# Attention into softplus layer: another order of PSUM pools, two weight loads into the `part` buffer, and casts of the first weights in later units

## The chip, the cores and the metric

The kernel is one launch on one core of a Trainium2 chip. The metric is device time in microseconds; the kernel before was run three times. The engines are named as in the profile: PE (TensorE matmuls), PEld (its weight loads), DVE (VectorE), ACT (ScalarE), POOL (GpSimd) and SP (SyncE, which issues DMAs). Each engine runs its own list of instructions in order and waits on semaphores for the others.

## The reference

Three layers run one after the other, on 1152 tokens (2 batches of 576) with 512 features.

```
attention:  q,k rotated; scores = (q_rot @ k_rot^T)/sqrt(64); P = exp(scores - max);
            out = (P / (sum P + 1e-9)) @ v            # 2 batches, 8 heads, 576 rows, 64 features
x         = out transposed to (1152, 512)
layer 1:    h = x @ w_in (512x2048); g = max(h,0) + log1p(exp(-|h|)); x = g @ w_out (2048x512)
layer 2:    tokens with x @ w_skip > 0: expert e = argmax(x @ w_gate); x += gate * relu(x @ w1[e]) @ w2[e]
```

The weights arrive as 64-bit floats and are decoded on the chip; inputs to matmuls are kept as a high and a low part (`xh`, `xl`; the two halves of a `w` tile), and a product is three matmuls.

## The kernel before

**Attention** (`Attention.run`) goes over units `(b, hp, u)`: batch, pair of heads, a chunk of 128 rows. In each unit PE makes scores `s`, DVE takes their maximum `m`, ACT makes `P` by exp, PE transposes `P` into PSUM tiles `t`, ACT and DVE copy these to `pt`, and PE multiplies `pt` with the values (`pv`, from `vd` and `vr`). When a chunk is done, PE transposes the normalisation (`t..n`), ACT copies it to `rb`, DVE multiplies `x = pv * rb`, and POOL splits `x` into `xh` and `xl`. There is one PSUM buffer for `pv`, so the next chunk's first `pv` matmul waits until DVE has read the last one. The order is written out by hand within a unit.

Beside the units run **jobs on the first weights** of layer 1. `W_AT` gives, for weight `(f, x)` (f a slice of 128 hidden columns; x is 0 for `w_in`, 1 for `w_out`), the numbers of the units at whose end each job is issued: load, first decode, second decode, `high`, `low`. `decode` is three DVE instructions on 128x512 (raw to `wt`; lines 557, 558, 560), `high` is an ACT cast of `wt` into `w` (line 565), `low` a DVE subtraction (line 569). The jobs of later weights are placed by `Moe1.weights`, in program order with a scheduler.

**Layer 1** walks over steps (chunk of tokens, f). `hidden` issues 12 matmuls of 512 columns per PSUM tile of 512 tokens (`h000` is chunk 0, f=0; `h010` f=1; line 591), then on ACT `y`=abs, `r`=relu, exp, `d`, `u`=ln (lines 604 to 614), on DVE three additions into `d` and `r` (615 to 617), on ACT the cast `gh` and on DVE `gl`. `out_mm` adds three matmuls for each of four token tiles into `acc` (line 629), and runs two steps behind `hidden`: the PE order is h000, h010, h020, h030, acc for f=0, h040, acc for f=1, h050, and so on. `hidden` has two PSUM buffers (pool `hp`), so h020 waits until ACT has read h000 twice (`y`, `r`).

Pools take memory in the order in which they are opened, and layer 1's lie where attention's were: the first writer of a new tile waits for the last reader or writer of the old one. Before, the PSUM pools of attention are opened `ps_s`, `ps_t`, `ps_pv`, and h000 lies in a slot of `ps_t` whose last tile is `t13n1`, the normalisation of the last chunk. In both kernels the tile `w2` lies where the values `vd` were, so that the cast `w2<-wt20` on ACT waits for the first `pv131<-pt131,vd1` matmul. The raw weights of 512 KB go through a ring `st` of two buffers. Layer 2 (`Moe2`) follows on the same engines.

Of the kernel before, what the change touches and what calls it, by code (L numbers as in the profile page):

```python
# [11 lines left out]
F32 = mybir.dt.float32  # L12
# [8 lines left out]
PSUM = bass.MemoryType.PSUM  # L21
# [17 lines left out]
SMALL = {1: ("l0",), 2: ("x0", "h0"), 3: ("t0", "r0"), 4: ("l1",), 5: ("x1", "h1"), 6: ("t1", "r1")}  # L39

W_AT = (
    ((0, 0), (18, 24, 25, 25, 26)), ((0, 1), (20, 26, 27, 27, 28)), ((1, 0), (25, 28, 29, 29, 30)),
    ((1, 1), (27, 30, 31, 31, 32)), ((2, 0), (29, 32, 33)), ((3, 0), (31, 34, 35)), ((2, 1), (33, 36, 37)),
)

WARM = (15, 4, 4, 3, 6, 3)

# [481 lines left out]
class Moe1:  # L529
# [6 lines left out]
        self.w, self.raw, self.t = {}, {}, {}  # L536


    def load(self, f, x):
        raw = self.raw[f, x] = self.st.tile([128, 512], mybir.dt.int64, name=f"raw{f}{x}", tag="st", bufs=2)  # L540
        fs = slice(128 * f, 128 * f + 128)
        if x == 0:
            src = self.w_in[:, fs].rearrange("(k p) n -> p k n", p=128)
            self.nc.sync.dma_start(raw.rearrange("p (k n) -> p k n", k=4), src)
        else:
            self.nc.sync.dma_start(raw, self.w_out[fs, :])
# [23 lines left out]

    def weights(self, f, x, wp, bufs, after):
        if (f, x) not in self.t:
            self.load(f, x)
            with after():
                self.decode(f, x, 0)
                self.decode(f, x, 1)
        with after():
            self.high(f, x, wp, bufs)
            self.low(f, x)
# [814 lines left out]
def const_views(ct):  # L1394
    return dict(
        ident=ct[:, 0:128], iota=ct[:, 128:256], wts=ct[:, 272:280], row1=ct[:, 280:289],
        far=ct[:, 289:290],
    )


def rope_views(cr):
    return dict(
        cos=cr[:, 0:256], sin=cr[:, 256:512], cosr=cr[:, 512:576], sinr=cr[:, 576:640],
    )
# [11 lines left out]
def attention_moe_moe_kernel(ctx: ExitStack, tc, q, k, v, w_in, w_out, w_skip, w_gate, w1, w2, tab, out):  # L1416
    nc = tc.nc

    def pool(stack, name, bufs=1, space=None, **kw):
        if space is not None:  # L1420
            kw["space"] = space
        return stack.enter_context(tc.tile_pool(name=name, bufs=bufs, **kw))
# [10 lines left out]
    with ExitStack() as s1:  # L1433
        xp = pool(s1, "xp")
        xh = xp.tile([128, 4, NTOK], F32R, name="xh")
        xl = xp.tile([128, 4, NTOK], F32R, name="xl")
        st = pool(s1, "st")
        moe1 = Moe1(nc, w_in, w_out, xh, xl, st)
        with ExitStack() as s2:
            nat, wq, wp, wk = pool(s2, "nat"), pool(s2, "wq"), pool(s2, "wp"), pool(s2, "wk")  # L1440
            ps = [pool(s2, "ps_s", 2, PSUM), pool(s2, "ps_t", 3, PSUM), pool(s2, "ps_pv", 1, PSUM)]
            cr = nat.tile([128, 640], F32, name="cr")
            nc.scalar.dma_start(cr, tab[:, 0:640])
            nc.scalar.dma_start(ct, tab[:, 640:930])
            cst = const_views(ct)
            cst.update(rope_views(cr))
            att = Attention(tc, q, k, v, cst, xh, xl, (nat, wq, wp, wk, *ps))

            def side(i):
                for (f, x), at in W_AT:  # L1450
                    for k, job in enumerate((moe1.load, moe1.decode, moe1.decode, moe1.high, moe1.low)[: len(at)]):
                        if at[k] == i:
                            job(f, x, **({"z": k - 1} if 0 < k < 3 else {"wp": wa, "bufs": 2} if k == 3 else {}))

            att.run(side)
# [8 lines left out]
        moe2.ring = [(wa, 2), (wc, 4)]  # L1464
        psa, accb = pool(ctx, "psa", 1, PSUM), pool(ctx, "accb", 2, PSUM)
        with ExitStack() as s2:
            gq, gp = pool(s2, "gq"), pool(s2, "gp")
            ring = [(wa, 2), (pool(s2, "wb0"), 3), (pool(s2, "wb1"), 2), (wc, 4)]
            tp = pool(s2, "tp")
            hp, accp = pool(s2, "hp", 2, PSUM), pool(s2, "accp", 3, PSUM)  # L1470
            cf = tp.tile([128, 512], F32, name="cf", tag="x2", bufs=5)[:, 0:256]
            nc.scalar.dma_start(cf, tab[:, 930:1186])
            nc.vector.tensor_copy(cb, cf)

            part = tp.tile([128, 4, 512], F32, name="part")
            ranges = ((0, 0, 6), (1, 0, 16), (2, 6, 16), (3, 6, 16))
            steps = [(ph, ci, f) for ph, (ci, f0, f1) in enumerate(ranges) for f in range(f0, f1)]
            due, pend, accs = [], [], {}
# [39 lines left out]
            for ph, ci, f in steps:  # L1518
# [20 lines left out]
                if (ph, f) in EARLY:  # L1539
                    c = EARLY.index((ph, f))  # L1540
                    raw = st.tile([128, 1024], F32, name=f"wr{c}", tag="st", bufs=2)
# [26 lines left out]
    with ExitStack() as s1:  # L1568
        wp, xp, ws = pool(s1, "wr"), pool(s1, "xp2"), pool(s1, "ws")
# [4 lines left out]
        ps = pool(s1, "ps_x", 2, PSUM), pool(s1, "ps_y", 1, PSUM), ((accb, "acc"), (pool(s1, "ps_h", 2, PSUM), "mh"))  # L1574
# [48 lines left out]
```

## Time and profile before

| what | value |
|---|---|
| median of 3 runs | 492.97 us (492.56 to 493.24) |
| the profiled execution | 493.06 us |
| its span | 491.2 us |
| mean granted PE clock | 0.998 |
| PE, DVE, ACT, POOL busy | 96%, 76%, 68%, 27% of the span |

The span is what the trace covers; about 1.9 us of the execution's own time lie around it. PE is busy nearly always, so that what counts is where PE has gaps, and which engine ends them.

### The profile page before, as it was taken

How to read it: one execution, taken by the hardware profiler on the slowest of the kernel's cores; microseconds unless marked ns; L12 is line 12 of the kernel's file. 1: busy time of each engine (PE TensorE's matmuls, PEld its weight loads, DVE VectorE, ACT ScalarE, POOL GpSimd, SP SyncE). 2: the span in 40 equal slices, each digit the busy share in tenths (PEclk: the TensorE clock that was granted, in tenths of full speed). 3: DMA queues.
4: the chain of work that ended last, by engine and by line, in shares of the span. 5: the costliest groups of instructions: out<-in, count | busy, mean ns of one | idle time of the engine just before them, and what ended most of it. 6: DMA issues, size and time to landing. Idle time of an engine off the chain costs nothing. (4 is left out here: it accounts for less than half of the span.)

```text
span 491.2 us, 8838 instructions
## 1 busy us (share of the span) xinstructions
PE 471.3 (96%) x3054; PEld 382.1 (78%) x3055; DVE 371.8 (76%) x699; ACT 332.3 (68%) x782; POOL 130.6 (27%) x166
## 2 busy tenths in 40 slices
PE   7999999999999999999999999999999999999994
PEld 3777777766777678999998898899897768677683
DVE  7666776688996796799988995454886688979563
ACT  2667776676877677876678677765685458957550
POOL 0966785766131400000000000000110152551002
PEclk9999999999999999999999999999999999999999
DMA  7477547458462240223344241420335545895231
GB/s 186 152 194 195 121 123 200 95 161 208 101 177 77 97 129 1 87 63 113 125 129 125 91 129 44 140 75 2 99 100 203 228 111 194 285 311 224 78 120 39
DMA packets 41509, 65.49 MB, mean 133 GB/s; under 512 B 9087, under 2 KB 23679, under 8 KB 41456
## 3 DMA queue, kind: packets, MB, share of 16 engines
q1 hardware_dynamic: 38480, 59.99, 40.0%
q0 software_dynamic: 1344, 4.20, 2.7%
q10 hardware_dynamic: 1632, 0.66, 0.6%
q8 instruction: 26, 0.43, 0.4%
q14 instruction: 27, 0.22, 0.1%
HBM read 67.32 MB, written 6.76 MB: 151 GB/s over the span
## 5 line engine op out<-in xcount | busy, mean ns | idle before, releaser
L591 PE MATMUL h<-xh,w 128*128 128x320 f32 (+2 forms) x464 | 104.2, 309 | 0.8 <-ACT rb L96 0.8
L629 PE MATMUL acc<-w,gh 128*128 128x512 f32 x288 | 80.8, 397 | 1.3 <-ACT gh L619 1.3
L591 PEld LDWEIGHTS h<-xh,w 128*128 128x128 f32 x464 | 78.1, 188 | 4.7 <-ACT rb L96 1.1
L591 PE MATMUL h<-xl,w 128*128 128x320 f32 (+2 forms) x232 | 69.2, 308 | 0.0
L270 DVE TENSOR_REDUCE m<-s 128x1 f32<-128x576 f32 x64 | 48.0, 754 | 19.5 <-PE s L261 16.1
L629 PEld LDWEIGHTS acc<-w,gh 128*128 128x128 f32 x288 | 51.8, 188 | 12.0 <-ACT gh L619 3.2
L283 ACT ACTIVATE P<-s,m 128x576 f32<-128x576 f32 x64 | 47.6, 749 | 12.3 <-DVE m L270 10.7
L705 POOL TENSOR_SCALAR sc<-lg 128x2 f32<-128x2 f32 (+1 forms) x3 | 0.9, 293 | 201.8 <-DVE lg L688 201.8
L973 DVE TENSOR_TENSOR ws<-raw,ws 128x1024 fp32r<-128x1024 f32 x42 | 49.4, 1219 | 6.6 <-ACT ws L966 6.1
L604 ACT ACTIVATE y<-h 128x320 f32<-128x320 f32 (+2 forms) x58 | 25.4, 438 | 41.1 <-PE h L591 39.9
L352 PE MATMUL t<-ct,P 128*128 128x128 f32 x288 | 45.5, 277 | 2.5 <-ACT pt L96 2.5
L629 PE MATMUL acc<-w,gl 128*128 128x512 f32 x144 | 45.9, 392 | 0.0
L966 ACT CAST ws<-raw 128x1024 fp32r<-128x1024 f32 x42 | 42.0, 1051 | 5.2 <-DMA raw<-in_moe_w_dram 5.0
L620 DVE TENSOR_TENSOR gl<-r,gh 128x256 fp32r<-128x256 f32 (+2 forms) x42 | 25.8, 614 | 26.0 <-ACT gh L619 25.8
L261 PE MATMUL s<-ks,qs 128*128 128x288 f32 x224 | 43.7, 317 | 1.8 <-ACT P L283 1.7
L591 PEld LDWEIGHTS h<-xl,w 128*128 128x128 f32 x232 | 43.2, 188 | 2.0
L352 PEld LDWEIGHTS t<-ct,P 128*128 128x128 f32 x288 | 33.6, 140 | 9.6 <-issue 3.5
L96 ACT COPY pt<-t 128x384 f32<-128x384 f32 x60 | 28.1, 480 | 18.0 <-PE t L352 17.9
L396 PE MATMUL pv<-pt,vr 128*64 128x256 f32 (+1 forms) x256 | 37.1, 412 | 0.0
L638 PE MATMUL y<-ws,hT 128*128 128x512 f32 (+1 forms) x150 | 37.0, 392 | 0.0
L261 PEld LDWEIGHTS s<-ks,qs 128*128 128x128 f32 x224 | 31.6, 189 | 6.6 <-ACT P L283 3.6
L638 PE MATMUL mh<-ws,xgT 128*128 128x512 f32 x132 | 36.6, 418 | 0.0
(305 smaller groups left out, 946.1 us busy)
## 6 DMA issues: line engine op xcount, KB each, us to landing
raw<-in_moe_w_dram SPq DMA_DIRECT2D x56, 512.0 KB
raw<-in_moe_w_in_dram SPq DMA_DIRECT2D x16, 512.0 KB
raw<-in_moe_w_out_dram SPq DMA_DIRECT2D x16, 512.0 KB
sraw<-in_moe_w_dram SPq DMA_DIRECT2D x16, 512.0 KB
ks<-kT SPq DMA_DIRECT2D x28, 288.0 KB
qs<-qT SPq DMA_DIRECT2D x28, 128.0 KB
wr<-in_moe_w_dram SPq DMA_DIRECT2D x5, 512.0 KB
x2d<-x SPq DMA_DIRECT2D x9, 256.0 KB
```

The costliest lines, as they stand in the source:

```text
L96: self.nc.scalar.copy(out, in_)
L261: nc.tensor.matmul(ps[:, c, 0:288], lhsT=qs[:, a, uc], rhs=ks[:, a, x, 288 * c : 288 * c + 288], start=x == 0, stop=x == 1,)
L270: self.last = nc.vector.tensor_reduce(st["m"][:, a : a + 1], st["ps"][a][:, :, 0:288], axis=AX.XY, op=ALU.max, negate=True)
L283: nc.scalar.activation(P[:, 576 * a : 576 * a + 576].rearrange("p (c n) -> p c n", c=2), ps[:, :, 0:288], AF.Exp, bias=m[:, a : a + 1], ac ...
L352: self.tail = nc.tensor.transpose(ps[:, 128 * i : 128 * i + 128], src, ident)
L396: nc.tensor.matmul(ps[r, 0:n], lhsT=v, rhs=pt[:, k, 0:n], start=i < 0, stop=i == 3, skip_group_check=True,)
L591: nc.tensor.matmul(ps[c][:, 0:m], lhsT=w[:, 0, x, 128 * k : 128 * k + 128], rhs=src[:, k, c0 + m * c : c0 + m * c + m], start=z == 0, stop ...
L620: self.last = nc.vector.tensor_sub(gl, r, gh.bitcast(F32))
L629: nc.tensor.matmul(acc[t], lhsT=g[x][:, 128 * j : 128 * j + 128], rhs=w[:, 1, y, :], start=f == f0 and z == 0, stop=f == f1 and z == 2,)
L638: mm()
L966: self.nc.scalar.copy(self.w[T, c][:, 0], self.raw[c] if raw is None else raw)
L973: self.nc.vector.tensor_sub(w[:, 1], self.raw[c] if raw is None else raw, w[:, 0].bitcast(F32))
```

## The change

It has three parts. (1) The PSUM pool `ps_t` is opened ahead of `ps_s`, so that the first `h` tiles lie where scores were. (2) Pool `tp` is opened ahead of `gq` and `gp`; a tile `px` of two raw buffers takes the memory that `part` uses later, and the raw loads of weights (5,0) and (4,1) are issued into it at the start of layer 1 and not through the ring `st`. (3) In `W_AT` two casts `high` and four subtractions `low` move to later units.

```
 W_AT = (
-    ((0, 0), (18, 24, 25, 25, 26)), ((0, 1), (20, 26, 27, 27, 28)), ((1, 0), (25, 28, 29, 29, 30)),
-    ((1, 1), (27, 30, 31, 31, 32)), ((2, 0), (29, 32, 33)), ((3, 0), (31, 34, 35)), ((2, 1), (33, 36, 37)),
+    ((0, 0), (18, 24, 25, 25, 27)), ((0, 1), (20, 26, 27, 28, 29)), ((1, 0), (25, 28, 29, 30, 31)),
+    ((1, 1), (27, 30, 31, 31, 33)), ((2, 0), (29, 32, 33)), ((3, 0), (31, 34, 35)), ((2, 1), (33, 36, 37)),
 )
+PX = ((5, 0), (4, 1))
...
-    def load(self, f, x):
-        raw = self.raw[f, x] = self.st.tile([128, 512], mybir.dt.int64, name=f"raw{f}{x}", tag="st", bufs=2)
+    def load(self, f, x, raw=None):
+        if raw is None:
+            raw = self.st.tile([128, 512], mybir.dt.int64, name=f"raw{f}{x}", tag="st", bufs=2)
+        self.raw[f, x] = raw
...
         if (f, x) not in self.t:
-            self.load(f, x)
+            if (f, x) not in self.raw:
+                self.load(f, x)
...
-            ps = [pool(s2, "ps_s", 2, PSUM), pool(s2, "ps_t", 3, PSUM), pool(s2, "ps_pv", 1, PSUM)]
+            ps_t, ps_s, ps_pv = pool(s2, "ps_t", 3, PSUM), pool(s2, "ps_s", 2, PSUM), pool(s2, "ps_pv", 1, PSUM)
...
+            tp = pool(s2, "tp")
             gq, gp = pool(s2, "gq"), pool(s2, "gp")
             ring = [(wa, 2), (pool(s2, "wb0"), 3), (pool(s2, "wb1"), 2), (wc, 4)]
-            tp = pool(s2, "tp")
             hp, accp = pool(s2, "hp", 2, PSUM), pool(s2, "accp", 3, PSUM)
+            px = tp.tile([128, 2, 512], mybir.dt.int64, name="px", tag="part")
+            for z, at in enumerate(PX):
+                moe1.load(*at, raw=px[:, z])
...
-            part = tp.tile([128, 4, 512], F32, name="part")
+            part = tp.tile([128, 4, 512], F32, name="part", tag="part")
```

The number behind a name in the rows of order below is only a count of tiles.

First place: ACT in attention, where chunk `t10n1` is normalised, before:

```order
L283 ACTIVATE P11m_1697,sm111_1698<-s11m0_1683,m11m_1694 128x576
L288 COPY P11m_1697<-P11m_1697 128x64
L565 CAST w0_1587<-wt01_1646 128x512
L96 COPY rb101_1727<-t10n1_1719 128x256
L96 COPY rb101_1727<-t10n1_1719 64x64 x2
```

and in the changed kernel (lines are some lower there by the added code):

```order
L285 ACTIVATE P11m_1696,sm111_1697<-s11m0_1682,m11m_1693 128x576
L290 COPY P11m_1696<-P11m_1696 128x64
L98 COPY rb101_1726<-t10n1_1718 128x256
L98 COPY rb101_1726<-t10n1_1718 64x64 x2
L98 COPY pt110_1613<-t1132_1722 128x3x128
L98 COPY pt111_1743<-t11m0_1748 128x4x64 x2
L285 ACTIVATE P110_1757,sm111_1697<-s1100_1738,m110_1753 128x576
L285 ACTIVATE P110_1757,sm111_1697<-s1101_1759,m110_1753 128x576
L569 CAST w0_1587<-wt01_1645 128x512
```

The cast of weight (0,1) stood ahead of the two copies of `rb101`; now it stands behind two exps. On DVE the subtraction `w0<-wt00` now stands just ahead of the second decode of `wt01` and of `x101`, and the subtraction `w0<-wt01`, which stood ahead of the next decodes, now stands behind two maxima.

Second place: PE at the end of attention (`t1312` is the last transposed `P`, `pv131` the last chunk's output). Before:

```order
L352 MATMUL t1311_2333<-ct_65,P131_2293 128x128 x3
L352 MATMUL t1312_2338<-ct_65,P131_2293 128x128 x3
L396 MATMUL pv131_2351<-pt131_2244,vd1_105 64x320 x2
L396 MATMUL pv131_2351<-pt131_2244,vr13_1782 64x320 x8
L316 MATMUL t13n1_2365<-ct_65,R131_2348 128x128 x3
L591 MATMUL h000_2441<-xh_74,w0_1587 128x512
L591 MATMUL h000_2441<-xl_75,w0_1587 128x512
```

In the changed kernel (the 12 matmuls of h000 begin right behind `t1312`, and these rows begin at the last of them):

```order
L596 MATMUL h000_2444<-xh_74,w0_1587 128x512
L596 MATMUL h010_2475<-xh_74,w1_1867 128x512
L596 MATMUL h010_2475<-xl_75,w1_1867 128x512
L596 MATMUL h010_2475<-xh_74,w1_1867 128x512 x2
L596 MATMUL h010_2475<-xl_75,w1_1867 128x512
L596 MATMUL h010_2475<-xh_74,w1_1867 128x512 x2
L596 MATMUL h010_2475<-xl_75,w1_1867 128x512
L398 MATMUL pv131_2351<-pt131_2244,vd1_105 64x320 x2
L398 MATMUL pv131_2351<-pt131_2244,vr13_1781 64x320 x8
L318 MATMUL t13n1_2365<-ct_65,R131_2348 128x128 x3
L596 MATMUL h010_2475<-xh_74,w1_1867 128x512 x2
```

All 12 matmuls of h000 and 8 of the 12 of h010 now stand ahead of `pv131`; before, all of them stood behind `t13n1`.

Third place: ACT at the same point of the program, before:

```order
L96 COPY pt131_2244<-t1312_2338 128x3x128
L565 CAST w2_2435<-wt20_1983 128x512
L565 CAST w3_2438<-wt30_2081 128x512
L565 CAST w2_2435<-wt21_2173 128x512
L96 COPY rb131_2369<-t13n1_2365 128x256
L96 COPY rb131_2369<-t13n1_2365 64x64 x2
L1472 DMA cf_2431<-in_constants_dram 128x256
L565 CAST w4_2507<-wt40_2503 128x512
L565 CAST w3_2438<-wt31_2512 128x512
L604 ACTIVATE y00_2454<-h000_2441 128x512
L606 ACTIVATE r00_2455<-h000_2441 128x512
L608 ACTIVATE y00_2454<-y00_2454 128x512
```

and in the changed kernel:

```order
L98 COPY pt131_2244<-t1312_2338 128x3x128
L569 CAST w2_2438<-wt20_1982 128x512
L569 CAST w3_2441<-wt30_2081 128x512
L609 ACTIVATE y00_2457<-h000_2444 128x512
L611 ACTIVATE r00_2458<-h000_2444 128x512
L569 CAST w2_2438<-wt21_2173 128x512
L613 ACTIVATE y00_2457<-y00_2457 128x512
L1482 DMA cf_2434<-in_constants_dram 128x256
L98 COPY rb131_2369<-t13n1_2365 128x256
L98 COPY rb131_2369<-t13n1_2365 64x64 x2
L617 ACTIVATE d00_2465<-y00_2457 128x512
L619 ACTIVATE u00_2459<-y00_2457 128x512
```

The casts `w2` and `w3` still come right behind the last `pt131` copy; `y00` and `r00` now stand right behind them, ahead of `rb131`, and the second cast of `w2`, and those of `w4` and `w3`, later. On DVE the subtraction `w2<-wt20` still is the first instruction behind the last `pt131` copy. From it up to and with the third addition `r01` (which the `gh` cast for f=1 waits for) there are 31 instructions before and 30 in the changed kernel; the set is the same but for one subtraction `w4<-wt41`, which now comes behind `r01`. From h100 on, layer 1 has the same order in both kernels, and so has what is executed of layer 2.

## Rows read from the trace of the kernel before

**Rows 1.** Busy time by stretch: PE, PEld, DVE, ACT, POOL, clock, DMA share, GB/s.

```profile
200.00:300.00 100.00, 100.00 (x566) 91.29 (x565) 88.79 (x139) 73.67 (x194) 0.00 (x0) 1.00 0.36 111
400.00:491.00 91.00, 84.01 (x549) 63.90 (x547) 66.20 (x83) 55.62 (x79) 24.51 (x14) 0.99 0.51 176
```

**Rows 2.** Timeline of chunk `t10n1` in attention: start, us, engine, line, operation, [idle before, releaser].

```profile
115.41 0.55 PE L316 MATMUL t10n<-ct,R 128*128 128x128 f32 x3
115.46 0.75 DVE L560 SCALAR_TENSOR_TENSOR wt<-raw,wt 128x512 uint32<-128x512 uint32 x1
...
116.24 0.62 ACT L565 CAST w<-wt 128x512 fp32r<-128x512 f32 x1 [1.17 <-DVE wt L560]
...
116.77 0.69 ACT L96 COPY rb<-t10n 128x256 f32<-128x256 f32 x3
117.28 0.76 DVE L270 TENSOR_REDUCE m<-s 128x1 f32<-128x576 f32 x1 [1.08 <-PE s L261]
...
117.96 0.48 DVE L405 TENSOR_TENSOR x<-pv,rb 128x320 f32<-128x320 f32 x1
...
118.50 0.65 PE L396 MATMUL pv<-pt,vd 128*64 128x256 f32 x4 [0.66 <-DVE x L405]
```

**Rows 3.** Busy time by stretch around it.

```profile
116.00:120.00 4.00, 3.08 (x25) 1.99 (x23) 2.88 (x7) 3.68 (x11) 3.92 (x5) 1.00 1.00 225
...
124.00:128.00 4.00, 3.11 (x26) 2.68 (x25) 3.97 (x9) 3.52 (x10) 2.34 (x4) 1.00 0.46 135
```

**Rows 4.** Timeline from the end of attention into layer 1.

```profile
160.87 0.76 PE L396 MATMUL pv<-pt,vd 128*64 128x320 f32 x4
...
161.67 1.66 ACT L565 CAST w<-wt 128x512 fp32r<-128x512 f32 x3 [0.42 <-PE pv L396]
162.32 1.29 DVE L569 TENSOR_TENSOR w<-wt,w 128x512 fp32r<-128x512 f32 x2 [1.64 <-ACT w L565]
...
163.71 0.55 PE L316 MATMUL t13n<-ct,R 128*128 128x128 f32 x3
...
165.09 0.50 PE L591 MATMUL h<-xh,w 128*128 128x512 f32 x1 [0.84 <-ACT rb L96]
...
175.88 0.39 PE L591 MATMUL h<-xh,w 128*128 128x512 f32 x1
```

**Rows 5.** Timeline: POOL's split of `x`, alone and beside DVE.

```profile
154.49 0.46 POOL L100 TENSOR_SCALAR xh<-x 128x320 fp32r<-128x320 f32 x1 [0.91 <-DVE x L405]
...
155.03 0.87 POOL L407 TENSOR_TENSOR xl<-x,xh 128x320 fp32r<-128x320 f32 x1
...
166.58 1.63 POOL L100 TENSOR_SCALAR xh<-x 128x320 fp32r<-128x320 f32 x1 [4.90 <-DVE x L405]
...
167.81 2.23 DVE L569 TENSOR_TENSOR w<-wt,w 128x512 fp32r<-128x512 f32 x2
...
168.30 1.20 POOL L407 TENSOR_TENSOR xl<-x,xh 128x320 fp32r<-128x320 f32 x1
...
169.59 0.88 POOL L776 TENSOR_SCALAR gt<-least 128x40 f32<-128x40 f32 x3
```

**Rows 6.** Timeline: DVE's two waits for raw loads, and its `r01`.

```profile
171.09 0.43 DVE L557 TENSOR_SCALAR wt<-raw 128x512 uint32<-128x512 uint32 x1 [1.04 <-DMA raw<-in_moe_w_in_dram]
...
177.18 0.43 DVE L557 TENSOR_SCALAR wt<-raw 128x512 uint32<-128x512 uint32 x1 [0.38 <-DMA raw<-in_moe_w_out_dram]
...
181.25 0.69 DVE L617 TENSOR_TENSOR r<-r,d 128x512 f32<-128x512 f32 x1
```

**Rows 7.** Timeline of PE: first `acc` matmuls for f=0 and for f=1.

```profile
176.90 2.14 PE L629 MATMUL acc<-w,gh 128*128 128x512 f32 x8 [0.64 <-ACT gh L619]
...
182.65 2.14 PE L629 MATMUL acc<-w,gh 128*128 128x512 f32 x8
```

**Rows 8.** Busy time from DVE's `w2<-wt20` to its `r01`.

```profile
162.32:181.83 19.51, 18.04 (x84) 13.81 (x81) 18.01 (x31) 13.88 (x27) 3.83 (x7) 1.00 0.37 117
```

**Rows 9.** Timeline of SP: the raw load of weight (5,0).

```profile
167.12 0.37 SPq L544 DMA_DIRECT2D raw<-in_moe_w_in_dram  x1
```

More of the change, by code (lines that the diff above doesn't have):

```diff
@@ L1446, in attention_moe_moe_kernel @@
             cst.update(rope_views(cr))
-            att = Attention(tc, q, k, v, cst, xh, xl, (nat, wq, wp, wk, *ps))
+            att = Attention(tc, q, k, v, cst, xh, xl, (nat, wq, wp, wk, ps_s, ps_t, ps_pv))
             def side(i):
```

## The prediction, made before the changed kernel was run

> **What bounds the kernel now.** First the busy time by stretch: PE is busy without a gap over the 100 us of layer 1 after its start, and loses 7 us in the last 91 us [rows 1]. A delay or a gain ahead of 200 us is therefore carried to the end, if layer 2 absorbs nothing of it (I take that it doesn't; nothing in layer 2 is moved). So only PE's gaps ahead of 200 us can be won or made, and I read the timeline at the two places that the change moves: one chunk of attention at 115 to 119 us, and the passage into layer 1 from 160 to 185 us. Every time below that is not "before" is an estimate made from these rows.
>
> **Attention: the casts in other units.** The subject is `x`, since PE's next `pv` waits for it: `pv` starts at 118.50, released by DVE's `x` of 117.96, which ran 0.48 [rows 2]. `x` needs `rb`, three copies of together 0.69 from 116.77, and these stood behind a cast of 0.62 at 116.24, which waited 1.17 for DVE's decode. `t10n` itself was there at 115.41 + 0.55 = 115.96 [rows 2]. In the changed order the cast stands behind, so `rb` can run from about 116.0 to 116.7. On DVE one subtraction now goes ahead of the decode: 0.60, which is what a second instruction of such a pair adds (1.29 for two [rows 4], 0.69 for one [rows 6]). Decode at 116.06, `x` from about 116.7 to 117.2, `pv` from 117.3 where PE is free. That is up to 1.2 earlier, but PE has only 4.00 - 3.08 = 0.92 idle in this stretch to give back [rows 3]. **Term 1: -0.9.** DVE fills with this subtraction what was idle (1.08 before `m` at 117.28 [rows 2]), so that its total does not grow. Bounds: PE's other gap nearby, 4.00 - 3.11 = 0.89 [rows 3], lies where DVE is busy 3.97 of 4 us; if the freed DVE time closes that too, -1.8. If the subtraction ahead of `x` is held up by POOL as one of the pair below is (0.94/2 = 0.47), -0.45.
>
> **PSUM order: what it removes.** Before, h000 waits for `rb` and starts at 165.09, with 0.84 of PE idle ahead of it [rows 4]. Where scores lay, the last reader is long done, and h000 starts right behind the last transposes, at about 160.8. That much is a pure gain: h000 is 4.3 earlier.
>
> **What it moves.** The same 20 hidden matmuls now stand ahead of `pv131`. One costs (175.88 - 165.09)/47 = 0.230, from the first and the last of 48 [rows 4]; 20 of them 4.6. So `pv131` starts at about 165.4 where it was 160.87: 4.5 later. Behind `pv131` hangs the cast `w2` on ACT, at 161.67 before, released by `pv` [rows 4]; and on it DVE's `w2` subtraction, at 162.32, released by the cast [rows 4]. Both are 4.5 later: 166.2 and 166.8. Queued behind them on ACT are `y00` and `r00`, and on DVE all of the decoding of w4, w3 and w5 and the additions for f=0 and f=1. PE earns 4.3 us of early matmuls and DVE stands still for as long.
>
> **Whether DVE then sets the end.** The last instruction that matters on DVE is `r01`: ended at 181.25 + 0.69 = 181.94 [rows 6], and the `acc` matmuls for f=1 came 0.71 later, at 182.65, with no gap on PE [rows 7]. So before, DVE was just in time there, with nothing in hand. From `w2` to `r01` it took 181.94 - 162.32 = 19.62, of which 19.51 - 18.01 = 1.50 was idle [rows 8], chiefly the two waits for raw loads, 1.04 and 0.38 [rows 6]. Those two go (next part), and one subtraction (0.60) moves behind `r01`: 17.5 are left. From 166.8 this ends at 184.3, and `acc` for f=1 starts at 185.0 and not at 182.65: +2.4. DVE may start a little earlier than by this sum, since h000 meets a running PE; I take **term 2: +2.2**.
>
> **The bounds of term 2.** In the 17.5 there is a collision. DVE's pair at 167.81 took 2.23 and not 1.29, while POOL split `x` in 1.63 and 1.20, which took 0.46 and 0.87 at 154.49 and 155.03 [rows 5]. DVE lost 0.94. In the changed kernel POOL's split again falls into DVE's dense run (behind `x131`, at about 172), so I keep it; without it +1.3. Upward: POOL's three `gt` instructions (0.88 [rows 5]) may lie beside DVE as well; by half their time, 0.44, and with the split costing DVE POOL's whole 0.46 + 0.87 = 1.33, it is +3.0.
> The Trainium skill ("SBUF — State Buffer", section "Who interferes with whom") says that a DVE instruction with two SBUF inputs and a GpSimd instruction that reads SBUF exclude each other through a shared port, the later one blocked for all of the other. By that rule the loss would be 1.33 and the sum below 0.4 higher; the trace agrees that both sides suffer, and shows 0.94.
>
> **The loads into `part`.** They wait for the last matmul that reads `vr13`, at about 165.4 + 2.8 = 168.2 (`pv131` takes up to `t13n1`, 163.71 - 160.87 [rows 4]). A load took 171.09 - 167.12 = 3.97 from issue to DVE's use [rows 6, 9], so the first lands at about 172.2. DVE wants it as its 12th instruction, at about 173.9, and the second two microseconds and more after that. They cost nothing: 1.7 of DVE work cover them, and if that cover is gone each 0.1 of lateness is 0.1 at `r01`. Through the ring the load would wait for `wt40` to be decoded, about 171.2, and land at 175.2, 1.3 too late; so this part earns what the sum leaves out. On SP the load of (5,1) stands behind both; it needs a ring buffer that DVE frees at about 171, and is wanted at 178. The moved pool and the extra tile add no instruction.
>
> **The rest of the passage.** h020 waits for `r00`: casts of 1.66/3 = 0.55 each [rows 4] from 166.2, then `y00` and `r00`, to about 168.5; PE gets there at 165.4 + 3.4 + 0.9 = 169.7 (`pv131` and `t13n1` took 163.71 + 0.55 - 160.87 [rows 4], then 4 matmuls of h010). No wait. h030 waits for `r01` of ACT, at about 172.8 against 172.4. The `acc` matmuls for f=0 come at about 177.4, against 176.90 with 0.64 idle [rows 7]; all of that lies inside the wait at f=1 and isn't added.
>
> **Sum.** -0.9 + 2.2 = +1.3 on the profiled execution's 493.06 us, which is 0.09 above the median of the three runs. On the median that is 494.3 us. About 0.2% (1 us) is what a measurement of this kernel can tell from no change.
>
> **The rivals.**
> - *No change to be seen.* The mechanism is as above, but POOL's split does not cost DVE its 0.94 (+1.3), or attention gives both gaps back (-1.8): with one of the two +0.4, with both -0.5, so 492.5 to 493.4. For it: POOL was the one that lost more in rows 5. Against: DVE is denser there than before. With half of either it is +0.8, still unseen. Chance 0.40.
> - *Faster.* The cast `w2` does not hang on `pv131` any more, because the pools that were reordered put `w2` elsewhere. Then ACT and DVE start as before, `r01` is not late, and PE keeps what it loses now, 0.84 ahead of h000 and 0.64 ahead of `acc` [rows 4, 7]: -1.5 - 0.9 = -2.4, 490.6 us. It decides from the point where DVE's `w2` starts before about 164.6 (the 2.2 given back). Against: the cast follows the same copies in both orders, and its old memory is still that of the values. Chance 0.09.
> - *Much slower.* The split and `gt` block DVE wholly (+3.0) and attention returns 0.45: +2.5, 495.5 us. Against: the measured pair lost less. Chance 0.13, within the slower side.
> - *Weights late.* The loads into `part` are behind on SP, and DVE waits at `wt50` again, 1.04 as before [rows 6]: +2.3, 495.3 us. Chance 0.05.
>
> **Numbers.** The forecast, +1.3 with its own spread of +1.0 to +1.9, has 0.33; with the two slower rivals slower has 0.51, no visible change 0.40, faster 0.09. The range leaves out the faster rival and the worst of the slower ones: 492.4 to 495.3.
>
> **What would show it.** Right: h000 at about 160 on PE behind the last transposes, no gap; DVE idle for some 6 us ahead of `w2`, released by ACT; a PE gap of about 2 us ahead of `acc` for f=1, released by ACT's `gh`, where before there was none; no wait of DVE for a raw load there; the pair gap at 116 to 120 gone. Wrong: DVE's `w2` near 162, `r01` ending within a few tenths of its old time, or gaps in attention that stay.

## The result, and the profile after

The changed kernel took 495.87 us (median of 6, 495.12 to 496.11), the kernel before 493.01 us in the same comparison: +2.86 us, a ratio of 1.0061 with a 95% interval of 1.0048 to 1.0074. The forecast was 494.3 us, +1.3: the right side, less than half of the size, and the measured time lies above the range of 492.4 to 495.3. The profiled execution took 495.73 us, its span is 493.9 us (491.2 before).

By stretch (columns as in [rows 1]) the changed kernel shows:

```profile
100.00:140.00 40.00, 36.66 (x277) 27.79 (x274) 35.34 (x66) 29.28 (x78) 18.53 (x26) 1.00 0.61 164
...
160.00:180.00 20.00, 17.84 (x91) 13.03 (x90) 13.82 (x27) 12.91 (x27) 6.20 (x11) 1.00 0.34 111
180.00:200.00 20.00, 18.46 (x90) 15.52 (x89) 16.27 (x26) 15.22 (x29) 0.00 (x0) 1.00 0.08 27
200.00:300.00 100.00, 100.00 (x561) 90.86 (x560) 87.60 (x138) 75.96 (x200) 0.00 (x0) 1.00 0.36 111
...
400.00:494.00 94.00, 86.69 (x557) 65.26 (x556) 68.14 (x85) 58.18 (x83) 25.12 (x15) 0.98 0.50 174
```

PE is again busy without a gap from 200 to 300 us, so nearly all that is lost was lost ahead of 200 us. The kernel before had this in two of the stretches:

```profile
160.00:180.00 20.00, 18.39 (x90) 13.51 (x89) 16.91 (x31) 13.78 (x28) 5.43 (x11) 1.00 0.35 113
180.00:200.00 20.00, 20.00 (x97) 16.77 (x96) 14.48 (x24) 16.07 (x33) 0.00 (x0) 1.00 0.08 27
```

PE was busy for 18.39 + 20.00 us of the 40 from 160 to 200 us; here it is 17.84 + 18.46.

The passage into layer 1, the answer to [rows 4 to 7], is this in the changed kernel's timeline:

```profile
161.07 0.47 PE L596 MATMUL h<-xh,w 128*128 128x512 f32 x1
...
165.81 0.76 PE L398 MATMUL pv<-pt,vd 128*64 128x320 f32 x4
...
166.62 1.14 ACT L569 CAST w<-wt 128x512 fp32r<-128x512 f32 x2 [4.78 <-PE pv L398]
167.26 1.29 DVE L573 TENSOR_TENSOR w<-wt,w 128x512 fp32r<-128x512 f32 x2 [6.00 <-ACT w L569]
...
172.12 1.43 POOL L102 TENSOR_SCALAR xh<-x 128x320 fp32r<-128x320 f32 x1 [9.86 <-DVE x L407]
...
173.26 0.58 DVE L561 TENSOR_SCALAR wt<-px 128x512 uint32<-128x512 uint32 x1
...
173.64 0.94 POOL L409 TENSOR_TENSOR xl<-x,xh 128x320 fp32r<-128x320 f32 x1
...
173.76 0.96 DVE L1483 CAST cb<-cf 128x256 bf16<-128x256 f32 x1
...
177.85 2.11 PE L634 MATMUL acc<-w,gh 128*128 128x512 f32 x8 [2.16 <-ACT gh L624]
...
183.76 0.68 DVE L622 TENSOR_TENSOR r<-r,d 128x512 f32<-128x512 f32 x1
...
185.15 2.11 PE L634 MATMUL acc<-w,gh 128*128 128x512 f32 x8 [1.54 <-ACT gh L624]
```

h000 starts behind the last transposes with no wait. `pv131` comes 4.74 later; ACT's cast `w2` has waited 4.78 for it, and DVE 6.00 for the cast. `r01` ends at 184.44, and PE stands 2.16 ahead of `acc` for f=0 and 1.54 ahead of f=1, both times for `gh`. No load of raw weights holds DVE up. DVE loses time beside POOL's split of `x` again: the `cb` cast took 0.96 here, beside POOL's `xl` of 173.64, and 0.29 in the kernel before:

```profile
167.61 0.29 DVE L1473 CAST cb<-cf 128x256 bf16<-128x256 f32 x1
```

The place in attention, the answer to [rows 2]:

```profile
115.73 0.55 PE L318 MATMUL t10n<-ct,R 128*128 128x128 f32 x3
115.78 0.74 DVE L573 TENSOR_TENSOR w<-wt,w 128x512 fp32r<-128x512 f32 x1
115.94 3.41 POOL L139 TENSOR_TENSOR rot<-rot,rt 128x512 f32<-128x512 f32 x2
...
116.31 0.69 ACT L98 COPY rb<-t10n 128x256 f32<-128x256 f32 x3 [0.92 <-PE t10n L318]
...
116.45 1.77 DVE L564 SCALAR_TENSOR_TENSOR wt<-raw,wt 128x512 uint32<-128x512 uint32 x1
...
118.14 0.48 DVE L407 TENSOR_TENSOR x<-pv,rb 128x320 f32<-128x320 f32 x1
...
118.67 0.65 PE L398 MATMUL pv<-pt,vd 128*64 128x256 f32 x4 [1.00 <-DVE x L407]
```

The changed trace runs 0.31 late ahead of this place already: `x` of the chunk before starts at 104.99, and at 104.68 in the kernel before. With 0.31 taken off, `rb` came 0.77 earlier than before, since the cast is out of its way, but `x` only 0.13 and `pv` only 0.14 earlier, and PE waits 1.00 for `x` where it waited 0.66. The row that was not foreseen is the decode at 116.45: 1.77 where it took 0.75.

To compare traces, the starts of three instructions and the end of the span are enough. *Attention* below is from DVE's `x` at 104.68 (before) to that of 159.80, *passage* from there to PE's `acc` for f=1 (182.65), *rest* from there to the end of the span. What lies ahead of 104.68 is the same program in all kernels, and its time differs by up to 1.2 us from one execution to the next.

| kernel | attention | passage | rest | timed, ratio to before (95% interval) |
|---|---|---|---|---|
| before | 55.12 | 22.85 | 308.55 | |
| changed | 55.39 | 24.77 | 308.75 | 1.0061 (1.0048 to 1.0074) |
| changed, once more | 55.36 | 24.78 | 308.97 | 1.0063 (1.0049 to 1.0077) |
| wat_only | 55.37 | 23.28 | 308.78 | 1.0022 (1.0013 to 1.0031) |
| ps_only | 55.22 | 23.55 | 308.56 | 1.0031 (1.0019 to 1.0043) |
| px_only | 55.57 | 25.49 | 308.82 | 1.0064 (1.0051 to 1.0077) |
| ps_px | 54.96 | 24.78 | 308.88 | 1.0057 (1.0044 to 1.0070) |
| vd_first | 55.02 | 23.67 | 308.91 | 1.0030 (1.0019 to 1.0041) |
| vd_r0 | 55.18 | 21.55 | 308.74 | 0.9993 (0.9984 to 1.0002) |
| w2_own | 57.18 | 19.99 | 308.60 | 0.9994 (0.9983 to 1.0005) |
| wat_low26 | 53.76 | 23.02 | 308.68 | 0.9991 (0.9982 to 1.0000) |
| after_low26 | 53.75 | 24.79 | 308.97 | 1.0023 (1.0014 to 1.0032) |
| best | 53.76 | 21.55 | 308.89 | 0.9963 (0.9950 to 0.9977) |

By the traces the change costs +0.27 in attention and +1.92 in the passage, 2.19 of the 2.86.

### The profile page after: what moved, and what is told of

It reads as the page before. It is cut to its first block, busy times and chain, and to the rows that moved or that the text cites. A ratio compares the mean times of both kernels' runs of the same rounds, so it can differ in the third digit from the quotient of the medians.

```text
span 493.9 us, 8837 instructions
## 1 busy us (share of the span) xinstructions
PE 471.3 (95%) x3055; PEld 382.0 (77%) x3055; DVE 371.9 (75%) x699; ACT 332.1 (67%) x782; POOL 128.6 (26%) x166
```

## The experiments

Each expectation was written before its run. "Theory M" in it is the explanation that the traces had suggested by then, "the prediction's step" is what the prediction had said, and a rival is another explanation. The edits are shortened.

**The three parts, one at a time.** Four kernels on one chip, beside the kernel before (492.72 us): `wat_only` has the new `W_AT` alone, `ps_only` the new order of PSUM pools, `px_only` the loads into `part`, `ps_px` both of the last two.

```
wat_only:  -W_AT (old)    +W_AT (new)
ps_only:   pools opened ps_s, ps_t, ps_pv    ->  ps_t, ps_s, ps_pv
px_only:   tp opened ahead of gq and gp;  +px = tp.tile(..., tag="part");  +moe1.load(*at, raw=px[:, z])
ps_px:     ps_only and px_only together
```

> The kernel before, with the new unit numbers of the casts alone. Theory M (from the two traces): DVE's decode now starts behind the moved subtraction, meets POOL's rope instructions and runs 1.8 us where it took 0.75, so the x that frees pv's buffer is no earlier, and a later DVE wait adds a little: +0.2 to +0.4 us, the same within the measurement. The prediction's own step: -0.9 us. Rival R (the casts are the larger part of the +2.9): +1 us or more.

Measured 493.83 us, +1.1, which is the size that rival R gave. By its trace attention lost 0.25, as in the changed kernel, where the prediction's step had a gain of 0.9: in attention theory M holds and that step fails. The decode is again slow and late:

```profile
116.13 1.76 DVE L560 SCALAR_TENSOR_TENSOR wt<-raw,wt 128x512 uint32<-128x512 uint32 x1
```

The passage lost 0.43 as well, which theory M had smaller: DVE waits 0.88 for a raw load where it had waited 0.38 [rows 6]. In the changed kernel that wait doesn't exist.

> The kernel before, with the PSUM pools in the new order alone. PE's order is that of the changed kernel: 20 hidden matmuls ahead of pv131. Theory M: DVE starts about 4.4 us later than before, but up to r01 it has only 27 instructions here, since those of weight (5,1) stand behind it: r01 ends at about 182.4, acc for f=1 at 183.1, +0.5 us (0 to 1.2). By the prediction's step on the loads (through the ring a load of weight (5,0) lands 1.3 us too late) it would be worse than with the loads into part: +2.5 to +3.5 us.

Measured 494.14 us, +1.4, a little above theory M's bound of 1.2; the passage in the trace, +0.70, lies in it. The step on the loads fails: without the loads into `part` the passage is 1.2 shorter than with them (24.78 in `ps_px`), and DVE waits for no raw load ahead of `r01`.

> The kernel before, with the loads into part's buffer alone. Theory M: since the raw weights are there earlier, nine decoding instructions go ahead of r00 on DVE (r00 is the 26th instruction from w2 on, the 22nd before); acc for f=0 starts at about 178.2 and not at 176.9, and PE carries that on: +1.3 us. Rival (the loads only take away DVE's waits of 1.04 and 0.38 us): -0.6 us or no change.

Measured 495.79 us, +3.1: slower than theory M said, and on the other side from its rival. The profiled execution was the slowest of the six (496.93). The rows of `px_only`, on PE and of the clock:

```profile
179.08 3.13 PE L634 MATMUL acc<-w,gh 128*128 128x512 f32 x8 [1.82 <-ACT gh L624]
182.01 1.67 PE L634 MATMUL acc<-w,gl 128*128 128x512 f32 x4
...
186.28 1.98 PE L634 MATMUL acc<-w,gh 128*128 128x512 f32 x8
```

```profile
178.00:180.00 2.00, 0.92 (x4) 0.78 (x5) 2.00 (x4) 1.56 (x3) 0.00 (x0) 0.97 0.55 131
180.00:182.00 2.00, 2.00 (x6) 1.53 (x5) 1.93 (x4) 1.69 (x3) 0.00 (x0) 0.50 0.32 131
182.00:184.00 2.00, 2.00 (x8) 1.55 (x7) 1.04 (x3) 1.77 (x5) 0.00 (x0) 0.68 0.00 0
```

`x` of the last chunk but one was 0.99 later than before in this execution, `acc` for f=0 2.18 later: 1.2 of the passage, which is theory M's 1.3. The other 1.45 lie between the two `acc` starts, 7.20 where it was 5.75, and there the clock is lower: behind the wait of 1.82 the granted clock (the last column but two) is 0.50 from 180 to 182, that is 1.2 GHz where it was 2.4, and the 8 matmuls took 3.13 that take 2.14 [rows 7]. Five of its six timed runs have a mean clock of 0.991 or 0.992 and took 495.62 to 496.93, the sixth 0.996 and 494.97; those of the kernel before have 0.994 to 0.998.

> The changed kernel with the old unit numbers of the casts. Theory M: DVE's order from w2 to r01 is that of the changed kernel and starts some 4.4 us later than before: +1.9 to +2.4 us, so nearly all of the change. Rival R: about +1.5 us or less, the casts being the rest.

Measured 495.38 us, +2.7, passage +1.93: theory M. The changed kernel, which has the casts' new units as well, takes 0.43 more in attention (55.39 against 54.96) and 0.2 to 0.4 more in the timed runs: what `wat_only` lost on its own, 1.1, is not added in full.

**What the passage hangs on.** Three kernels on the base of `ps_px`. `vd_first` puts the first `pv131` matmuls ahead of h000, since h000 may be issued only behind `att.tail`; `vd_r0` also holds back the decoding of three weights until the addition `r00` is issued; `w2_own` keeps PE's order and gives `w2` and `w3` memory in which no attention tile lay, so that their casts can run during attention.

```
vd_first:  in pv_mm:    +if i < 0:
                        +    self.tail = mm
vd_r0:     in hidden:   +self.r = nc.vector.tensor_add(r, r, d)
                        +self.r0 = self.r0 or self.r
           the call of moe1.weights:
                        -... else nullcontext()
                        +... else tc.issue_after(moe1.r0.ins) if f > 2 else nullcontext()
w2_own:    +w2p = pool(s1, "w2p")                  # opened ahead of attention's pools
           pool wb0 with 1 buffer and not 3
           -wb, n = ring[SLOT[fw]]
           +wb, n = (w2p, 2) if fw in (2, 3, 11, 12) else ring[SLOT[fw]]
```

> The changed kernel with the old unit numbers of the casts and one difference: layer 1's first hidden matmuls may be issued only behind the first matmuls of pv131 (those that read vd). PE's order is then t1312, five pv131 rows, h000, the rest of pv131, t13n1, h010. Theory M (the loss is that the cast w2 hangs on pv131, which stood behind 20 hidden matmuls): the cast and DVE start as before, at about 161.7 and 162.3, h000 at about 162.3, r01 ends at about 180, acc for f=1 at about 180.8 where it was 182.65: -1.5 to -2 us against the kernel before. Rival (early hidden matmuls or the loads into part cost time in themselves, whatever order pv131 has): +1.5 us or more, as with ps_px.

Measured 494.44 us, +1.7: 1 us better than `ps_px`, but on the rival's side, and far from theory M's -1.5. DVE did start at its old time (162.65, against 162.32). But DVE's timeline has two new waits:

```profile
162.65 1.29 DVE L575 TENSOR_TENSOR w<-wt,w 128x512 fp32r<-128x512 f32 x2 [1.63 <-ACT w L571]
...
169.01 0.49 DVE L409 TENSOR_TENSOR x<-pv,rb 128x320 f32<-128x320 f32 x1 [1.39 <-ACT rb L98]
...
172.16 0.43 DVE L563 TENSOR_SCALAR wt<-px 128x512 uint32<-128x512 uint32 x1 [1.56 <-DMA px<-in_moe_w_in_dram]
...
182.41 0.68 DVE L624 TENSOR_TENSOR r<-r,d 128x512 f32<-128x512 f32 x1
```

`x131` waits 1.39 for `rb`, the decode of (5,0) 1.56 for its load. Both hang on the last half of `pv131`, which now stood behind h000, and the three later decodes stand ahead of `r01`. Theory M was too narrow: not the cast alone counts, but all that hangs on `pv131`, and the order of DVE's instructions behind it.

> vd_first, and the decoding of weights (5,0), (4,1) and (5,1) is issued only behind the addition r00. Theory M: r00 is DVE's 15th instruction from w2 on and r01 the 29th, and PE is no longer kept waiting by either: acc for f=1 at about 180.6, -2 us, a little better than vd_first. Rival (DVE's order does not matter once it starts at 162.3): the same as vd_first.

Measured 492.31 us against 492.78: no change from the kernel before that can be told (-0.5), and 2.1 less than `vd_first`. The passage took 21.55 in the trace, 1.3 less than before and 2.1 less than `vd_first`: DVE's order does matter, and PE has no gap from h010 to f=1. Of the 2.1 the larger part is the wait of 1.56 for the load of (5,0), which stood ahead of `r00` in `vd_first` and is gone here. The trace is of the fastest of twelve executions (491.30; the slowest took 493.95).

> ps_px with one difference: weights 2 and 3 (and 11 and 12) get two buffers that no attention tile used, so that the casts w2 and w3 wait for nothing of attention. PE's order is that of the changed kernel, 20 hidden matmuls ahead of pv131. Theory M (the loss is the cast behind pv131): the casts, the subtractions and part of the next decoding now run during attention, DVE has no wait of 6 us, PE no gap ahead of acc for f=0, and acc for f=1 starts at about 181 where it was 182.65: -1 to -1.8 us against the kernel before, -3.5 to -4.5 us against ps_px. Rival (the order of PE itself, or the loads into part that wait for vr, is the larger part): +0.5 us or more.

Measured 492.57 us against 492.92, no change that can be told, and some 3 us better than `ps_px`. In its timeline (ACT and DVE, then PE):

```profile
167.68 0.60 ACT L609 ACTIVATE y<-h 128x512 f32<-128x512 f32 x1 [4.82 <-PE pv L398]
...
169.30 0.69 DVE L573 TENSOR_TENSOR w<-wt,w 128x512 fp32r<-128x512 f32 x1 [7.01 <-ACT w L569]
...
172.31 0.68 DVE L622 TENSOR_TENSOR r<-r,d 128x512 f32<-128x512 f32 x1
...
180.26 0.68 DVE L622 TENSOR_TENSOR r<-r,d 128x512 f32<-128x512 f32 x1
```

```profile
176.46 1.98 PE L634 MATMUL acc<-w,gh 128*128 128x512 f32 x8
...
181.90 1.98 PE L634 MATMUL acc<-w,gh 128*128 128x512 f32 x8
```

PE has the changed kernel's order, and no wait ahead of either `acc`; the passage is the shortest of all, 19.99. The standstill behind `pv131` is still there: ACT waits 4.82 for it, now with `y00`, and DVE 7.01. But from its end to `r01` DVE has 18 instructions and not 30, as most of the rest ran during attention. So the 20 hidden matmuls ahead of `pv131` do no harm in themselves; what costs is the DVE work that has to wait behind them. The 2.9 us that the passage gained are no gain of the kernel: its attention took 57.18, 2.1 more, with the decodes now among maxima that PE waits for (what each of them costs there was not measured).

**What attention hangs on.** `wat_low26` is `wat_only` with the subtraction of weight (0,0) at its old unit; `after_low26` is the changed kernel with the same.

```
-    ((0, 0), (18, 24, 25, 25, 27)),
+    ((0, 0), (18, 24, 25, 25, 26)),
```

> The kernel before with the new unit numbers of the casts but for one subtraction, that of weight (0,0), which stays where it was. Theory M (with that subtraction ahead, DVE's decode came behind the start of POOL's rope instruction and was held up): the decode starts as before at about 115.5 and takes 0.75, x runs at about 116.7, pv at 117.4 to 117.6, with little or no gap of PE there: -0.9 us at that place, and -0.5 to -0.9 us at the end of attention. Rival (x is bound by something else): pv at 118.3 or later, as in wat_only, no gain.

Measured 492.41 us against 492.78 (-0.4), 1.4 better than `wat_only`. Its DVE, POOL and PE rows at the place:

```profile
115.72 0.74 DVE L560 SCALAR_TENSOR_TENSOR wt<-raw,wt 128x512 uint32<-128x512 uint32 x1
115.88 2.96 POOL L137 TENSOR_TENSOR rot<-rot,rt 128x512 f32<-128x512 f32 x2
...
117.03 0.49 DVE L405 TENSOR_TENSOR x<-pv,rb 128x320 f32<-128x320 f32 x1 [0.57 <-PE t11m L352]
...
117.58 0.65 PE L396 MATMUL pv<-pt,vd 128*64 128x256 f32 x4
```

The decode starts 0.16 ahead of POOL's instruction, and takes 0.74; `pv` waits for nothing. Attention took 53.76, -1.36. The passage, where DVE waits 0.78 and 0.83 for raw loads, gives 0.17 of it back. By the three stretches -1.06 is left, and the timed runs show -0.4; the last experiment comes back to this difference.

> The changed kernel with the one subtraction of weight (0,0) back at its old unit. Theory M: attention ends about 1.2 us earlier than in the changed kernel (1.0 of it from the decode that POOL no longer holds up), all of it is carried on, since the passage is timed from attention's end: about +1.6 us against the kernel before. Rival: the passage swallows it, +2.5 us or more.

Measured 494.18 us, +1.3, where the changed kernel had +2.9: the one number 27 cost it 1.6 us. The passage swallows nothing (24.79).

**The two together.**

> vd_r0 with the unit numbers of wat_low26. Theory M: the two gains add, since one lies in attention and the other in the passage: vd_r0 gave -0.5 and wat_low26 -0.4 in the timed runs, so -0.9 us; by their traces (1.3 in the passage, 1.1 in attention) up to -2.4 us. Rival (one takes away what the other gains): -0.5 us.

Measured 491.30 us against 492.92, 0.9963 (0.9950 to 0.9977): 1.6 us faster than the kernel before, some 4.5 faster than the changed one. Both stretches keep what they had alone (53.76, 21.55), so the two gains add.

**What one trace doesn't hold.**

> The changed kernel once more, unaltered, to see what of its +2.9 us the one trace does not hold: from the traces attention gives +0.27 and the passage +1.92, 2.2 together, and the start of the execution, which differs by 0 to 0.6 us between executions of whatever kernel, 0.3 more. If the rest is a part of the kernel, attention (first x at 104.7 to the last but one) and passage (to acc for f=1) take some tenths longer here than in the first trace, for instance with a lower granted clock behind one of PE's gaps, and the timed difference is again near +2.9. If it is chance of that comparison, the same two figures as before and a timed difference of +2.2 to +2.5 us.

Measured 496.01 us against 492.95: +3.1. Attention and passage are those of the first trace within 0.03, so the two traces give the same +2.2 for both together. Behind PE's wait the clock fell in this execution, where it hadn't in the first:

```profile
176.00:178.00 2.00, 0.77 (x3) 0.67 (x4) 2.00 (x5) 1.15 (x2) 0.10 (x2) 1.00 0.24 82
178.00:180.00 2.00, 2.00 (x7) 1.52 (x6) 2.00 (x5) 1.22 (x2) 0.00 (x0) 0.60 0.01 4
180.00:182.00 2.00, 2.00 (x7) 1.57 (x6) 2.00 (x5) 1.23 (x2) 0.00 (x0) 0.55 0.00 0
182.00:184.00 2.00, 2.00 (x11) 1.65 (x10) 2.00 (x5) 1.95 (x4) 0.00 (x0) 1.00 0.00 0
```

```profile
177.23 2.82 PE L634 MATMUL acc<-w,gh 128*128 128x512 f32 x8 [2.15 <-ACT gh L624]
179.85 1.91 PE L634 MATMUL acc<-w,gl 128*128 128x512 f32 x4
...
184.53 2.11 PE L634 MATMUL acc<-w,gh 128*128 128x512 f32 x8
```

Its cost is hidden here: the slow matmuls end when `gh` for f=1 comes, so the wait ahead of 184.53 is gone and the passage as long. The remaining 0.2 to 0.4 lie in the rest (308.75 and 308.97 against 308.55, but 308.56 to 308.97 over all kernels), and the profiled executions (495.73 and 495.32) lie below the medians of their kernel, that of the kernel before (493.06) above. The other runs bear on the last 0.5 us. In eleven of the twelve traces of altered kernels the timed difference lies 0.2 to 0.7 us above the sum of the three stretches (`ps_only` 1.42 against 0.81, `wat_low26` -0.37 against -1.06, `best` -1.62 against -2.32). A surplus that nearly all share points at the one trace of the kernel before, to which all are compared, as a little long in its stretches, and not at a cost of this change behind 185 us. No second trace of that kernel shows it; if it is so, the losses by stretches in the table are some tenths too small, and the gains as much too large.

## Why the prediction was half right

The forecast was +1.3, measured was +2.86. Of the 1.56 between them attention has 1.17 and the passage -0.28; 0.67 lies in neither (see the last experiment).

**Term 1, attention, -0.9, measured +0.27: this is the step that failed.** It read "Decode at 116.06, `x` from about 116.7": DVE's next instruction was moved by 0.60 and priced at its old 0.75. It had that price because it started at 115.46, ahead of POOL's rope instruction at 115.61, a row that I didn't look at (POOL in the kernel before):

```profile
115.61 2.97 POOL L137 TENSOR_TENSOR rot<-rot,rt 128x512 f32<-128x512 f32 x2
```

In the changed kernel the decode starts at 116.45, behind the subtraction, and so after POOL's first instruction, which a timeline that ends behind it shows by itself:

```profile
115.94 1.73 POOL L139 TENSOR_TENSOR rot<-rot,rt 128x512 f32<-128x512 f32 x1
```

POOL's first instruction ends at 117.67, the decode at 116.45 + 1.77 = 118.22, 0.55 later, nearly its own length: it stood still until POOL was done. `wat_low26` takes the subtraction away and gets the gain, by its trace even more than forecast (-1.36). The bound that I gave for this collision, 0.47, came from half of another pair; the collision cost 1.0, and the upper side of term 1 ended at -0.45.
The Trainium skill ("SBUF — State Buffer", section "Who interferes with whom") says that the order of issue decides which of the two is blocked, and that the other is blocked wholly. Here the traces agree: the decode took 0.75 with DVE 0.15 ahead, 1.77 with POOL 0.51 ahead. In the prediction I weighed that rule on the pair of [rows 5] alone, where the loss was smaller than its price, and did not ask which other pairs the change would put the other way round.

The collision has a second cost, in the next chunk, where the prediction had only a possible gain of 0.9 [rows 3]. DVE is still behind there, and PE waits 0.63 for its copy `pt` ahead of `tq`, where it had no wait before. First the row of the kernel before, then that of the changed one:

```profile
125.67 0.60 PE L174 MATMUL tq<-ct,rot 128*128 128x128 f32 x4
```

```profile
126.48 0.66 PE L176 MATMUL tq<-ct,rot 128*128 128x128 f32 x4 [0.63 <-DVE pt L100]
```

In `after_low26` this wait is gone. By it PE went from 0.14 early at the `pv` of 118.67 to 0.40 late at that of 129.75 (129.04 before), and 0.27 is left at the end of attention.

The step also took the cast for all that held `x` up. In [rows 2] `rb` was there at 116.77 + 0.69 = 117.46, and `x` started at 117.96, behind DVE's maximum `m` of 117.28. In the new order `x` stands ahead of that maximum (in `wat_low26` at 117.03, the maximum at 117.55). How much of the gain comes from this and how much from the cast was not separated.

**Term 2, the passage, +2.2, measured +1.92: right, by its own steps.** The last chunk but one was 0.58 later in the changed trace; with that taken off, h000 started at 160.5 (160.8 forecast), `pv131` at 165.2 (165.4), the cast at 166.0 (166.2), DVE at 166.7 (166.8), `r01` ended at 183.9 (184.3), `acc` for f=0 came at 177.3 (177.4) and for f=1 at 184.6 (185.0 by the sum, 184.85 as taken). The collision with POOL was there and cost DVE some 0.8 (0.58 and 0.96 for two instructions of 0.43 and 0.29), against 0.94. `w2_own` and `vd_r0` bear out the cause: with less of DVE's work behind the wait, or with DVE started at its old time and three decodes held behind `r00`, the passage is shorter than before.

**The loads into `part`: the reason was wrong, the number stood.** I wrote that they earn 1.3, since a load through the ring would come too late. `ps_only`, without them, has the shorter passage by 1.2, and no wait for a raw load ahead of `r01`: there the decodes of (5,1) stand behind `r01` and not ahead of it. The load that is there early lets its decodes go ahead of the additions for which PE waits. The sum was made from the changed kernel's own order, which holds this, so only the explanation fell; but for a reader who wants to know which part to keep, it is the more costly error.

**The rivals.** "Much slower" had the time (+2.5) by another way: POOL did not block more in the passage, but blocked one instruction in attention. "Weights late" did not happen in the changed kernel (it did in `vd_first`). The range ended at this rival's 495.3 and left "much slower" out, and its bounds for term 1, -1.8 to -0.45, held no loss at all.

## What to carry to other kernels

When an instruction on DVE is moved, look at what POOL runs at its new time, not only at what it waits for: a shift of 0.6 us that lets POOL go first cost 1.0. When an engine gets work earlier, list what hangs on the work that is pushed behind it, down to a cast on a third engine; and when data come earlier, see what then goes ahead in an in-order queue. In the passage the gain was not in starting PE earlier but in letting DVE reach in time the two additions that PE waits for.

## What the runs showed of the hardware

The granted clock fell to 1.2 GHz for some 3 us behind waits of PE of 1.82 (`px_only`), 2.15 (`after_again`) and 2.16 (`after_low26`), and did not behind waits of 2.16 and 2.13 in the changed kernel's first trace and `ps_px`: the same program at the same place went either way. Where another engine sets the next start, the slow matmuls cost nothing; where PE does, they cost 1.0 on 8 of them (`px_only`).

A DVE decode and POOL's rope instruction held each other up. The decode took 0.75 when it started 0.15 ahead, and 1.77 when POOL had started 0.51 ahead. POOL's first instruction, behind a DVE instruction by 0.15 or 0.16, took 1.74 in the kernel before and 1.73 in the changed one; its second took 2.97 - 1.74 = 1.23 where no decode ran beside it, and 3.41 - 1.73 = 1.68 behind the slow decode.

The time ahead of 104 us, the same instructions in all kernels, differed by up to 1.2 us between executions, so that a single trace's end tells less than its stretches: attention and passage agreed within 0.03 in the two traces of the changed kernel.
